# Linear attention and a token/channel mixer: work of batch 2 begun one block sooner, two relus moved to VectorE

## The chip, the cores and the metric

The kernel runs on one core of a Trainium2 chip. A core has five engines with a queue of instructions each: TensorE (PE in the profile; its weight loads are shown as PEld), VectorE (DVE), ScalarE (ACT), GpSimd (POOL) and SyncE (SP, which here only issues transfers). Each engine works through its own queue in order and waits on semaphores for the others. The metric is the time of one execution in device microseconds, as a median over runs; smaller is better.

## What is computed

Eight batches, eight heads, 576 positions, head size 64. Linear attention, whose output is rearranged to (8, 576, 512), and a mixer over positions and then over channels:

```python
def phi(x): return np.where(x > 0, x, np.exp(x) - 1.0) + 1.0
q_p, k_p = phi(q), phi(k)
kv  = einsum('bhsd,bhse->bhde', k_p, v);   z = sum(k_p, axis=2)
x   = einsum('bhsd,bhde->bhse', q_p, kv) / (einsum('bhsd,bhd->bhs', q_p, z) + 1e-6)
x   = x.transpose(0, 2, 1, 3).reshape(8, 576, 512)
h   = maximum(x.transpose(0, 2, 1) @ w_tok1, 0) @ w_tok2      # w_tok1: 576 x 256
u   = x + h.transpose(0, 2, 1)
out = u + maximum(u @ w_ch1, 0) @ w_ch2                        # w_ch1: 512 x 1536
```

## The kernel before

The 576 positions of a batch are split in nine groups of 64 (T = 9): four pairs, which make four tiles of 128 rows (r = 0 to 3), and a tail of 64 (r = 4). The tails of an even and an odd batch share one tile of 128 rows.

For each batch the steps are:
- `phi` (L144) for q and k, in two halves g of four heads each: an exp on ScalarE (`e`, L125), then on VectorE `y` = x + 1 (L131), min(e, 1) (L139) and max of the two (L140) into `qp` or `kp`. `y` has one buffer, `e` has four.
- `vcast` (L149): v to bf16 in `vs`, in two halves; the first on ScalarE, the second on VectorE.
- `kv` (L162): 72 small matmuls, 36 for each half of the heads, and two copies to `kvbd` on ScalarE.
- q transposed into `qT`: for batch 1 by TensorE (`qtr`, L190), from batch 2 on by two DMA transposes issued from SyncE (`qtr_dma`, L197).
- `nd` (L228), six times: four (or two) matmuls on TensorE, then den, reciprocal and a product on VectorE (L219, L221, L222), which give `x`.
- `mm1` (L242): ten matmuls of 128x512 and two relus on ScalarE. `mm2` (L253) for rows 0-1, 2-3 and the tail: matmuls, then an addition on VectorE (L273, L269) into `u` or `ut`. For batch 1 `mm2_half` (L276) does this with the addition of L293.
- u transposed into `uT`: by DMA (`utr_dma`, L457; the tail `utt`, L463), for batches 0 and 1 by TensorE.
- `mm3` (L469): 12 blocks mc of four 128x512 matmuls, each closed by a relu, on ScalarE (L482) or, with `dve=True`, on VectorE (L479), into `cr`. `mm3_tail` (L484) does the tail of two batches in three groups. `mm4` (L495): for each tile of rows t, three slots of four matmuls, then an addition on VectorE (L518, tail L528) into `o_sb`, stored by transfers that GpSimd issues (SyncE and ScalarE in the last pair).

The order is written out by hand. A block's `big` list (the slots) holds the mm3, mm3_tail and mm4 steps of one batch; `fill` holds pairs (slot, step) of later batches' work, and `run` (L668) calls each `big` step and behind it the fill steps of its slot. That order is the order in every engine's queue. Block 0 works on mm3 and mm4 of batch 0 and holds all of batch 1's attention; block 1 (L709-724) has 30 slots: 12 of mm3 for batch 1 (0 to 11), 3 of the tail (12 to 14) and 15 of mm4 (15 to 29, t = 4 to 8). It holds the attention of batch 2 and the phi of batch 3. Its first mm3 steps (mc 0 to 2) are half done before it begins. The dictionaries `at0`, `at1`, `AT3`, `AT` give the slots of the named steps.

On chip the accumulators come from two pools: four banks (`ps_big`) that mm3, mm3_tail and mm4 take in turn, and two buffers of two banks (`ps_sm`) for kv, nd, mm1, mm2. A step that needs a bank waits until the step that had it has been read out. `raw` (the loaded q, k, v) has two sets, one for even and one for odd batches; the six loads of batch n + 2 can go when batch n's have been read. `qp`, `kp` and `vs` have one buffer each.

Of the kernel before, what the change touches and what calls it, by code (L numbers as in the profile page):

```python
# [18 lines left out]
def kernel(  # L19
# [20 lines left out]
    nc = tc.nc  # L40
# [13 lines left out]
    NCH = DCH // 128  # L54
# [54 lines left out]
    def load(nm, n, c, gate=None):  # L109
        src_ = src[nm][n].rearrange("(j a) (p t) d -> (a p) j (t d)", a=2, t=T)  # L110
        js = slice(2 * c, 2 * c + 2)
        return after(nc.sync.dma_start(out=raw[nm, n % 2][:, js], in_=src_[:, js]), gate)
# [9 lines left out]
    def phi_exp(nm, n, j0, nj):  # L122
        f = raw[nm, n % 2][:, j0:j0 + nj].rearrange("p j f -> p (j f)")
        e = work.tile([128, 2 * TD], BF16, name="e", tag="e", bufs=4)[:, :nj * TD]
        nc.scalar.activation(out=e, in_=f, func=AF.Exp)  # L125
        live["e", j0] = e

    def phi_add(nm, n, j0, nj):
        f = raw[nm, n % 2][:, j0:j0 + nj].rearrange("p j f -> p (j f)")
        y = work.tile([128, 2 * TD], BF16, name="y", tag="y", bufs=1)[:, :nj * TD]  # L130
        nc.vector.tensor_scalar(out=y, in0=f, scalar1=1.0, scalar2=None, op0=ALU.add)  # L131
        for j in range(nj):
            live["y", j0 + j] = y[:, j * TD:]

    def phi_end(nm, n, j0, nj):
        c, i = divmod(j0, 2)
        dst = (kp if nm == "k" else qp)[:, c, :, i:i + nj]
        e, y = live["e", j0], live["y", j0][:, :nj * TD]
        nc.vector.tensor_scalar(out=e, in0=e, scalar1=1.0, scalar2=None, op0=ALU.min)  # L139
        nc.vector.tensor_tensor(  # L140
            out=dst.transpose([0, 2, 1, 3]), in0=e.rearrange("p (i t d) -> p i t d", i=nj, t=T),
            in1=y.rearrange("p (i t d) -> p i t d", i=nj, t=T), op=ALU.max)

    def phi(nm, n, c):  # L144
        phi_exp(nm, n, 2 * c, 2)
        phi_add(nm, n, 2 * c, 2)
        phi_end(nm, n, 2 * c, 2)

    def vcast(n, c, copy=nc.scalar.copy):  # L149
        js = slice(2 * c, 2 * c + 2)  # L150
        copy(out=vs[:, js, :, 0:D],  # L151
             in_=raw["v", n % 2][:, js].rearrange("p j (t d) -> p j t d", t=T))
# [9 lines left out]
    def kv(n, cs):  # L162
        b = n % 2
        ps = ps_sm.tile([128, 2, 512], FP32, name="kv_ps", tag="sm")[:, :, 0:2 * D1].rearrange(
            "p a (c e) -> p a c e", c=2)
        for c in cs:
            for t in range(T):
                for a, i in QUARTERS:
                    nc.tensor.matmul(out=ps[half[i], a, c], lhsT=kp[half[a], c, t, i],  # L169
                                     rhs=vs[half[a], 2 * c + i, t],  # L170
                                     start=(t == 0), stop=(t == T - 1))
        cs = slice(cs[0], cs[-1] + 1)
        for i in range(2):
            at = slice(i * D1, (i + 1) * D1)
            nc.scalar.copy(out=kvbd[b][half[i], cs, :, at].transpose([0, 2, 1, 3]),
                           in_=ps[half[i], :, cs])
# [13 lines left out]
    def qtr(n, c, put=nc.scalar.copy):  # L190
        tp = ps_sm.tile([128, 2, 8, 128], BF16, name="tp", tag="sm")
        for h, ts in enumerate(TS):
            qtr_mm(c, ts, tp[:, h])
        for h, ts in enumerate(TS):
            qtr_put(n, c, ts, tp[:, h], put)

    def qtr_dma(n):  # L197
        for a in range(2):
            nc.sync.dma_start_transpose(
                out=qT[n % 2][:, 2 * TD * a:2 * TD * (a + 1)].rearrange("p (f s) -> p f s", s=D),  # L200
                in_=qp[half[a]].rearrange("p c t i d -> p (c t i d)"))
# [26 lines left out]
    def nd(n, g, rs):  # L228
        nd_mm(n, g, rs)
        nd_end(n, g, rs)  # L230
# [215 lines left out]
    def w2_put(kt):  # L446
        nc.scalar.copy(out=w2p[:, TD * kt:TD * (kt + 1)].rearrange("k (t p) -> k t p", t=T),
                       in_=w2r[:, kt].transpose([0, 2, 1]))
# [8 lines left out]
    def utr_dma(n, rs):  # L457
        b = n % 2
        nc.sync.dma_start_transpose(
            out=uT[b][:, rs[0]:rs[0] + len(rs)].rearrange("p r j c -> p (r j) c"),  # L460
            in_=u[b][:, rs[0]:rs[0] + len(rs)].rearrange("p r d -> p (r d)"))
# [7 lines left out]
    def mm3(n, mc, kjs=range(NDM), dve=False):  # L469
        b = n % 2  # L470
        if kjs[0] == 0:
            part_of[mc] = ps_big.tile([128, 512], FP32, name="c_ps", tag="big")
        ps = part_of[mc]
        for kj in kjs:
            nc.tensor.matmul(out=ps, lhsT=wc1[:, kj, 128 * mc:128 * mc + 128],  # L475
                             rhs=uT[b][:, :, kj],
                             start=(kj == 0), stop=(kj == NDM - 1))
        if kjs[-1] == NDM - 1 and dve:
            nc.vector.tensor_scalar(out=cr[b][:, mc, :], in0=ps, scalar1=0.0, scalar2=None,  # L479
                                    op0=ALU.max)  # L480
        elif kjs[-1] == NDM - 1:
            nc.scalar.activation(out=cr[b][:, mc, :], in_=ps, func=AF.Relu)  # L482
# [49 lines left out]
    def prep_k(n, g, copy=nc.scalar.copy):  # L532
        phi("k", n, g)
        vcast(n, g, copy)

    def load_all(n, nms):
        if n < B:
            for nm in nms:
                for g in range(2):
                    load(nm, n, g)  # L540
# [51 lines left out]
    dve, act = nc.vector.tensor_copy, nc.scalar.copy  # L592
# [57 lines left out]
    def steps(n):  # L650

        out_ = [("kv", lambda: kv(n, range(2)))]
        if n == 1:
            puts = [nc.scalar.copy, nc.vector.tensor_copy if n == 1 else nc.scalar.copy]
            out_ += [(f"qt{c}", lambda c=c: qtr(n, c, puts[c])) for c in range(2)]
        for i, rs in enumerate(([0, 1], [2, 3], [4])):
            for g in range(2):
                out_.append((f"nd{i}{g}", lambda g=g, rs=rs: nd(n, g, rs)))
        out_.append(("mm1", lambda: mm1(n)))
        if n > 1:  # L660
            out_ += [("mm2a", lambda: mm2(n, [0, 1])), ("mm2b", lambda: mm2(n, [2, 3])),
                     ("mm2t", lambda: mm2(n, [R]))]
            out_ += [("uta", lambda: utr_dma(n, [0, 1])), ("utb", lambda: utr_dma(n, [2, 3]))]
            if n % 2:
                out_.append(("utt", lambda: utr_tail_dma(n // 2)))
        return out_

    def run(bigs, fill):  # L668
# [5 lines left out]
        for s, fn in fill:  # L674
            assert s < len(bigs)

    m3 = lambda n, k0=0: [lambda mc=mc: mm3(n, mc) for mc in range(k0, NCH)]
    m3t = [lambda i=i: mm3_tail(i) for i in range(3)]
    m4 = lambda p, ts: [lambda t=t, i=i: mm4(p, t, range(4 * i, 4 * i + 4))
                        for t in ts for i in range(3)]  # L680
# [6 lines left out]
    big = [lambda mc=mc: mm3(0, mc, range(2, 4)) for mc in range(3)] + \  # L687
# [4 lines left out]
    fill = [(2, mm2_first_tail)]  # L692
# [4 lines left out]
                 (en, lambda nm=nm, c=c: phi_end(nm, 1, 2 * c, 2))]  # L697
    late = [("vc", lambda: vcast(1, 0)), ("vc", lambda: vcast(1, 1, nc.vector.tensor_copy))]
    fill += [(16 + kt, lambda kt=kt: w2_put(kt)) for kt in range(NT)]
    first = steps(1)  # L700
    for nm, fn in first[1:3] + late + first[0:1] + first[3:]:
        fill += [(at0[nm], fn)]
# [7 lines left out]
    for mc in range(3):  # L710
        mm3(1, mc, range(0, 2))
    utr_tail(0)
    big = [lambda mc=mc: mm3(1, mc, range(2, 4)) for mc in range(3)] + m3(1, 3) + m3t + m4(0, [4, 5, 6, 7, 8])
    at1 = {"kv": 11, "nd00": 13, "nd01": 14, "nd10": 15, "nd11": 16, "nd20": 17, "nd21": 18,
           "mm1": 20, "mm2a": 21, "mm2b": 22, "mm2t": 24, "uta": 21, "utb": 22}
    fill = [(s, lambda g=g: phi("q", 2, g)) for g, s in ((0, 0), (1, 2))]
    fill += [(3, lambda: qtr_dma(2)), (3, lambda: load_all(3, "qkv"))]
    fill += [(s, lambda g=g: phi("k", 2, g)) for g, s in ((0, 4), (1, 6))]
    fill += [(8, lambda: vcast(2, 0)), (9, lambda: vcast(2, 1, nc.vector.tensor_copy))]
    fill += [(at1[nm], fn) for nm, fn in steps(2)]  # L720
    fill += [(s, lambda g=g: phi("q", 3, g)) for g, s in ((0, 19), (1, 23))]
    fill += [(24, lambda: qtr_dma(3)), (24, lambda: load_all(4, "qkv"))]
    fill += [(s, lambda g=g: prep_k(3, g)) for g, s in ((0, 25), (1, 27))]
    run(big, sorted(fill, key=lambda e: e[0]))

    AT3 = {"kv": 1, "nd00": 3, "nd01": 4, "nd10": 5, "nd11": 6, "nd20": 7, "nd21": 8,
# [3 lines left out]
    for n in range(2, B):  # L730
        p, b = divmod(n, 2)
        if b == 0:
            big = m3(n) + m4(p, [0, 1, 2, 3])
        else:
            big = m3(n) + m3t + m4(p, [4, 5, 6, 7, 8] if n + 1 < B else [8, 4, 5, 6, 7])
        fill = []
# [40 lines left out]
```

## Time and profile before

| | |
|---|---|
| time, median of 7 runs | 268.23 us (267.40 to 268.55) |
| the profiled execution's own time | 268.46 us |
| its span, first to last instruction | 266.7 us |
| granted clock of TensorE, mean | 0.997 |
| last slots of block 0: last kc step of mm4 for batch 0 ends | 50.85 us |
| block 1: first slot begins | 56.74 us |
| kv of batch 2 begins | 67.22 us |
| mm1 of batch 2 begins | 76.98 us |
| block 2: first slot begins | 89.32 us |
| kv of batch 3 begins | 91.14 us |
| loads of q of batch 2: issued, and time to landing | 36.6 and 37.0 us, 6.0 and 6.8 us |

Times within the execution are counted from the start of the span. In a timeline each row is a run of like instructions: start, duration, engine, line of the kernel, operation, what is written from what is read, size, count, and in brackets the idle time of the engine ahead of it and what ended that. TensorE starts the next matmul before the last one has left it, so its rows overlap, and the start-to-start distance is the pace; the same holds, less so, for VectorE and ScalarE. A few per cent of the matmul records are missing, which shows as a hole of one matmul's length in a row.

### The profile page before, as it was taken

How to read it: one execution, taken by the hardware profiler on the slowest of the kernel's cores; microseconds unless marked ns; L12 is line 12 of the kernel's file. 1: busy time of each engine (PE TensorE's matmuls, PEld its weight loads, DVE VectorE, ACT ScalarE, POOL GpSimd, SP SyncE). 2: the span in 40 equal slices, each digit the busy share in tenths (PEclk: the TensorE clock that was granted, in tenths of full speed). 3: DMA queues.
4: the chain of work that ended last, by engine and by line, in shares of the span. 5: the costliest groups of instructions: out<-in, count | busy, mean ns of one | idle time of the engine just before them, and what ended most of it. 6: DMA issues, size and time to landing. Idle time of an engine off the chain costs nothing.

```text
span 266.7 us, 5122 instructions
## 1 busy us (share of the span) xinstructions
PE 255.9 (96%) x2088; PEld 134.1 (50%) x2107; DVE 157.4 (59%) x309; ACT 133.0 (50%) x202; POOL 32.4 (12%) x54
## 2 busy tenths in 40 slices
PE   7998989999999999999999999999999999999992
PEld 3684445553744454445464554445554554444641
DVE  5764977469587876948674296938684272420121
ACT  5635764269808368525771358425870353036300
POOL 9720300110000200030001300030001300000000
PEclk9999999999999999999999999999999999999998
DMA  7999999253957695799999990671067500730042
GB/s 261 247 203 288 366 223 403 97 132 97 337 209 154 154 385 204 86 224 349 312 409 235 266 407 27 141 164 43 2 129 120 118 2 0 157 99 2 0 118 79
DMA packets 49927, 48.34 MB, mean 181 GB/s; under 512 B 30256, under 2 KB 35248, under 8 KB 49904
## 3 DMA queue, kind: packets, MB, share of 16 engines
q1 hardware_dynamic: 41824, 35.53, 45.9%
q0 software_dynamic: 7440, 11.44, 20.1%
q10 hardware_dynamic: 640, 1.05, 1.2%
q8 instruction: 16, 0.26, 0.4%
q14 instruction: 7, 0.06, 0.1%
HBM read 35.85 MB, written 9.44 MB: 170 GB/s over the span
## 4 chain that ended last, share of the span: by engine, by line
PE 80%; DVE 7%; DMA 4%; ACT 4%; issue 3%; POOL 0%; ACTq 0%; POOLq 0%
PE h_ps L501 32%; PE c_ps L475 21%; PE a_ps L248 5%; PE h_ps L261 4%; PE c_ps L489 4%; DMA uTt<-ut 4%; PE bank L545 3%; PE nd_ps L210 3%; PE kv_ps L169 2%; DVE y L131 2%; ACT cr L482 1%; ACT e L125 1%; DVE e L139 1%; DVE kp L140 1%; PE bank L363 1%
## 5 line engine op out<-in xcount | busy, mean ns | idle before, releaser
L475 PE MATMUL c_ps<-uT,wc 128*128 128x512 bf16 x384 | 91.3, 379 | 0.7 <-ACT uT L444 0.4
L482 ACT ACTIVATE cr<-c_ps 128x512 bf16<-128x512 f32 x93 | 54.4, 603 | 74.1 <-PE c_ps L475 74.0
L501 PE MATMUL h_ps<-wc,cr 128*128 128x512 bf16 x377 | 87.4, 379 | 0.5
L501 PEld LDWEIGHTS <-cr 128*128 128x128 bf16 x384 | 37.0, 98 | 42.0
L475 PEld LDWEIGHTS <-wc 128*128 128x128 bf16 x384 | 35.8, 98 | 37.8 <-issue 1.9
L518 DVE TENSOR_TENSOR o_sb<-h_ps,u 128x512 f32<-128x512 f32 x32 | 21.8, 688 | 27.3 <-PE h_ps L501 25.6
L523 POOL DMA_DIRECT2D out_dram<-o_sb x24 | 14.5, 609 | 156.1 <-DVE o_sb L518 156.1
L222 DVE TENSOR_TENSOR x<-nd_ps,den 128x512 bf16<-128x512 f32 (+1 forms) x42 | 25.3, 602 | 1.5
L139 DVE TENSOR_SCALAR e<-e 128x1152 bf16<-128x1152 bf16 x30 | 13.9, 463 | 12.5 <-ACT e L125 12.4
L125 ACT ACTIVATE e<-k_raw 128x1152 bf16<-128x1152 f32 x16 | 18.8, 1173 | 2.3 <-DMA k_raw<-in_k_dram 2.3
L273 DVE TENSOR_TENSOR u<-h_ps,x 128x1024 bf16<-128x1024 f32 x12 | 14.4, 1220 | 9.2 <-PE h_ps L261 9.2
L125 ACT ACTIVATE e<-q_raw 128x1152 bf16<-128x1152 f32 x16 | 18.6, 1161 | 1.1 <-DMA q_raw<-in_q_dram 1.1
L219 DVE TENSOR_SCALAR den<-nd_ps 128x8 f32<-128x8 f32 (+1 forms) x42 | 6.8, 163 | 19.3 <-PE nd_ps L210 18.7
L251 ACT ACTIVATE ar<-a_ps 128x512 bf16<-128x512 f32 x14 | 7.6, 594 | 18.1 <-PE a_ps L248 18.1
L210 PEld LDWEIGHTS <-qT 128*128 128x128 bf16 x140 | 11.4, 98 | 9.5 <-issue 0.2
L261 PE MATMUL h_ps<-ar,w2p 128*128 128x512 bf16 x57 | 15.6, 379 | 0.1
L210 PE MATMUL nd_ps<-kvbd,qT 128*128 128x130 bf16 x140 | 15.1, 223 | 0.0
L248 PE MATMUL a_ps<-x,w 128*128 128x512 bf16 x50 | 13.9, 379 | 0.3
L151 ACT CAST vs<-v_raw 128x1152 bf16<-128x1152 f32 x12 | 13.9, 1162 | 0.0
L528 DVE TENSOR_TENSOR o_sb<-h_ps,ut 128x512 f32<-128x512 f32 x4 | 2.8, 689 | 18.7 <-PE h_ps L501 18.7
L131 DVE TENSOR_SCALAR y<-q_raw 128x1152 bf16<-128x1152 f32 x16 | 12.4, 773 | 0.3
L140 DVE TENSOR_TENSOR qp<-e,y 128x1152 bf16<-128x1152 bf16 x16 | 12.1, 759 | 0.6
(102 smaller groups left out, 215.7 us busy)
## 6 DMA issues: line engine op xcount, KB each, us to landing
k_raw<-in_k_dram SPq DMA_DIRECT2D x16, 576.0 KB, 8.9
q_raw<-in_q_dram SPq DMA_DIRECT2D x16, 576.0 KB, 6.8
v_raw<-in_v_dram SPq DMA_DIRECT2D x14, 576.0 KB, 10.9
out_dram<-o_sb POOLq DMA_DIRECT2D x24, 256.0 KB, 3.8
wc<-in_moe_w_ch_dram POOLq DMA_DIRECT2D x8, 384.0 KB, 9.3
out_dram<-o_sb SPq DMA_DIRECT2D x10, 128.0 KB, 2.3
out_dram<-o_sb ACTq DMA_DIRECT2D x8, 128.0 KB, 2.6
out_dram<-o_sb POOLq DMA_DIRECT2D x6, 128.0 KB, 6.9
```

What stands on the lines that cost most here:

```text
L125: nc.scalar.activation(out=e, in_=f, func=AF.Exp)
L131: nc.vector.tensor_scalar(out=y, in0=f, scalar1=1.0, scalar2=None, op0=ALU.add)
L139: nc.vector.tensor_scalar(out=e, in0=e, scalar1=1.0, scalar2=None, op0=ALU.min)
L140: nc.vector.tensor_tensor(out=dst.transpose([0, 2, 1, 3]), in0=e.rearrange("p (i t d) -> p i t d", i=nj, t=T), in1=y.rearrange("p (i t d) ...
L210: nc.tensor.matmul(out=o[:, a], lhsT=qT[b][:, t0:t0 + 128], rhs=kvbd[b][:, c, a], start=True, stop=True)
L222: nc.vector.tensor_tensor(out=x[b][:, rs[0]:rs[0] + m, HG * D * g:HG * D * (g + 1)].rearrange("p r (h d) -> p r h d", h=HG), in0=v_[:, :, ...
L248: nc.tensor.matmul(out=ps[:, mt], lhsT=w1t[:, b, ms] if r == R else w1[:, r, ms], rhs=x[b][:, r, :], start=(r == 0), stop=(r == R))
L261: nc.tensor.matmul(out=ps[:, i], lhsT=w2v(kt, r, b), rhs=ar[b][:, kt, :], start=(kt == 0), stop=(kt == NT - 1 and not add))
L475: nc.tensor.matmul(out=ps, lhsT=wc1[:, kj, 128 * mc:128 * mc + 128], rhs=uT[b][:, :, kj], start=(kj == 0), stop=(kj == NDM - 1))
L482: nc.scalar.activation(out=cr[b][:, mc, :], in_=ps, func=AF.Relu)
L501: nc.tensor.matmul(out=ps, lhsT=crt[:, kc, :] if t == 8 else cr[b][:, kc, 128 * r:128 * r + 128], rhs=wc2[:, kc, :], start=(kc == 0), stop ...
L518: nc.vector.tensor_tensor(out=o, in0=ps, in1=u[b][:, r, :], op=ALU.add)
```

## The change

Three edits, none of which alters what is computed.

1. The two halves of phi of q of batch 2 move from slots 0 and 2 of block 1 to slot 21 of block 0, behind batch 1's last nd step (slot 20) and ahead of its mm1 (slot 21). The two transposing transfers of q of batch 2 and the six loads of batch 3 move from slot 3 of block 1 to slot 22 of block 0.
2. In block 1 the rest of batch 2 moves up: the phi of k from slots 4 and 6 to 0 and 2, the casts of v from 8 and 9 to 4 and 5, kv from 11 to 7, the nd steps from 13, 14, 15, 16, 17, 18 to 9 to 14, mm1 from 20 to 16, mm2 from 21, 22, 24 to 17, 18, 20 with the transfers of u. Batch 3's phi of q goes from slots 19 and 23 to 19 and 21, its transposes and the loads of batch 4 from 24 to 22, its phi of k and casts from 25 and 27 to 24 and 26.
3. The relus of mc 4 and mc 7 of batch 1 go from ScalarE (L482) to VectorE (L479).

In the queues this means: TensorE has the same instructions, with kv, nd, mm1 and mm2 of batch 2 further ahead among the mm3 and mm4 steps. GpSimd's and SyncE's queues hold the same instructions in the same order. ScalarE's two exps of q of batch 2 stand behind the w2p copies of block 0 and ahead of batch 1's mm1 relus. VectorE's six instructions of that phi stand behind the last nd step of batch 1 and ahead of the first two output additions of batch 0 (L518); in block 1 the relu of mc 4 stands ahead of the cast of v's second half, the relu of mc 7 behind it.

```diff
     fill += [(16 + kt, lambda kt=kt: w2_put(kt)) for kt in range(NT)]
+    fill += [(21, lambda g=g: phi("q", 2, g)) for g in range(2)]
+    fill += [(22, lambda: qtr_dma(2)), (22, lambda: load_all(3, "qkv"))]
     first = steps(1)
...
-    big = [lambda mc=mc: mm3(1, mc, range(2, 4)) for mc in range(3)] + m3(1, 3) + m3t + m4(0, [4, 5, 6, 7, 8])
-    at1 = {"kv": 11, "nd00": 13, "nd01": 14, "nd10": 15, "nd11": 16, "nd20": 17, "nd21": 18,
-           "mm1": 20, "mm2a": 21, "mm2b": 22, "mm2t": 24, "uta": 21, "utb": 22}
-    fill = [(s, lambda g=g: phi("q", 2, g)) for g, s in ((0, 0), (1, 2))]
-    fill += [(3, lambda: qtr_dma(2)), (3, lambda: load_all(3, "qkv"))]
-    fill += [(s, lambda g=g: phi("k", 2, g)) for g, s in ((0, 4), (1, 6))]
-    fill += [(8, lambda: vcast(2, 0)), (9, lambda: vcast(2, 1, nc.vector.tensor_copy))]
+    big = [lambda mc=mc: mm3(1, mc, range(2, 4)) for mc in range(3)] + [lambda mc=mc: mm3(1, mc, dve=mc in (4, 7)) for mc in range(3, NCH)] + m3t + m4(0, [4, 5, 6, 7, 8])
+    at1 = {"kv": 7, "nd00": 9, "nd01": 10, "nd10": 11, "nd11": 12, "nd20": 13, "nd21": 14,
+           "mm1": 16, "mm2a": 17, "mm2b": 18, "mm2t": 20, "uta": 17, "utb": 18}
+    fill = [(s, lambda g=g: phi("k", 2, g)) for g, s in ((0, 0), (1, 2))]
+    fill += [(4, lambda: vcast(2, 0)), (5, lambda: vcast(2, 1, nc.vector.tensor_copy))]
     fill += [(at1[nm], fn) for nm, fn in steps(2)]
-    fill += [(s, lambda g=g: phi("q", 3, g)) for g, s in ((0, 19), (1, 23))]
-    fill += [(24, lambda: qtr_dma(3)), (24, lambda: load_all(4, "qkv"))]
-    fill += [(s, lambda g=g: prep_k(3, g)) for g, s in ((0, 25), (1, 27))]
+    fill += [(s, lambda g=g: phi("q", 3, g)) for g, s in ((0, 19), (1, 21))]
+    fill += [(22, lambda: qtr_dma(3)), (22, lambda: load_all(4, "qkv"))]
+    fill += [(s, lambda g=g: prep_k(3, g)) for g, s in ((0, 24), (1, 26))]
```

## The prediction

> **What bounds the kernel.** The page first: its parts 1 and 4.
>
> ```profile
> span 266.7 us, 5122 instructions
> ...
> PE 255.9 (96%) x2088; PEld 134.1 (50%) x2107; DVE 157.4 (59%) x309; ACT 133.0 (50%) x202; POOL 32.4 (12%) x54
> ...
> PE 80%; DVE 7%; DMA 4%; ACT 4%; issue 3%; POOL 0%; ACTq 0%; POOLq 0%
> ```
>
> TensorE is the bound. The diff neither adds nor removes a matmul, so it can only win or lose places where TensorE stands still. I therefore read TensorE's timeline from the end of batch 0's block to the first slots of batch 2's.
>
> ```profile
> 56.74 9.98 PE L475 MATMUL c_ps<-uT,wc 128*128 128x512 bf16 x42
> 67.22 0.78 PE L169 MATMUL kv_ps<-vs,kp 64*64 64x65 bf16 x72 [0.51 <-ACT vs L151]
> ...
> 89.32 1.89 PE L475 MATMUL c_ps<-uT,wc 128*128 128x512 bf16 x8
> 91.14 1.07 PE L169 MATMUL kv_ps<-vs,kp 64*64 64x65 bf16 x72
> ...
> 117.59 0.78 PE L169 MATMUL kv_ps<-vs,kp 64*64 64x65 bf16 x72
> 118.30 1.90 PE L475 MATMUL c_ps<-uT,wc 128*128 128x512 bf16 x8
> ```
>
> The pace of a 128x512 matmul is (1.89 - 0.38) / 7 = 0.216 (0.38 is the mean of one on the page), so four are 0.863. An undisturbed kv, batch 4's, takes 118.30 - 117.59 = 0.71, and 0.09 passes in front of it. Against that:
> - the 42 matmuls at 56.74 should take 41 x 0.216 + 0.38 = 9.22 and take 9.98. The starts of the single ones put the missing 0.76 ahead of mc 7 (61.64, 0.15 late), mc 9 (63.67, 0.30) and mc 11 (65.69, 0.30);
> - kv of batch 2 (67.22) starts 0.67 behind the last matmul's slot, 0.58 beyond the usual 0.09;
> - kv of batch 3 (91.14) takes 1.07 instead of 0.78: 0.28 lost in its middle.
>
> Together 1.62 us. Between them there is only 0.26 at 80.5, where mm2a waits for the relu of mm1; that distance isn't altered. ScalarE shows what holds block 1 up:
>
> ```profile
> 57.42 0.60 ACT L482 ACTIVATE cr<-c_ps 128x512 bf16<-128x512 f32 x1
> 57.91 1.17 ACT L125 ACTIVATE e<-q_raw 128x1152 bf16<-128x1152 f32 x1
> 58.96 1.09 ACT L482 ACTIVATE cr<-c_ps 128x512 bf16<-128x512 f32 x2
> 59.92 1.18 ACT L125 ACTIVATE e<-q_raw 128x1152 bf16<-128x1152 f32 x1
> 60.97 1.11 ACT L482 ACTIVATE cr<-c_ps 128x512 bf16<-128x512 f32 x2
> ...
> 65.94 1.23 ACT L151 CAST vs<-v_raw 128x1152 bf16<-128x1152 f32 x1
> ```
>
> From 57.4 to 69 it has no gap. One relu moves it on by 0.48, an exp or a cast by 1.05. With four banks, mc 7 needs the relu of mc 3, which ends 61.57; mc 9 and mc 11 need those of mc 5 and mc 7; kv needs the cast that ends 67.17. Then VectorE:
>
> ```profile
> 46.71 0.42 DVE L222 TENSOR_TENSOR x<-nd_ps,den 128x256 bf16<-128x256 f32 x1
> 50.40 1.29 DVE L518 TENSOR_TENSOR o_sb<-h_ps,u 128x512 f32<-128x512 f32 x2 [3.27 <-PE h_ps L501]
> 52.14 0.69 DVE L293 TENSOR_TENSOR u<-h_ps,x 128x512 bf16<-128x512 f32 x1 [0.45 <-PE h_ps L288]
> ...
> 59.10 0.46 DVE L139 TENSOR_SCALAR e<-e 128x1152 bf16<-128x1152 bf16 x1 [1.82 <-ACT e L125]
> 59.60 0.76 DVE L140 TENSOR_TENSOR qp<-e,y 128x1152 bf16<-128x1152 bf16 x1
> 60.39 0.76 DVE L131 TENSOR_SCALAR y<-q_raw 128x1152 bf16<-128x1152 f32 x1
> ...
> 90.91 0.76 DVE L140 TENSOR_TENSOR kp<-e,y 128x1152 bf16<-128x1152 bf16 x1
> ```
>
> Idle for 3.27 ahead of 50.40; the last row is batch 3's kp, ready at 91.67, which kv of batch 3 waits for.
>
> **Part 1: phi of q of batch 2 into block 0.** On ScalarE two exps, 2 x 1.05, go behind the w2p copies (end 42.99), where nothing runs until 49.32. Their input is issued at 36.56 and 37.05 and lands 6.0 and 6.8 later, 42.6 and 43.9. So they run from 43.0 to 45.2: cost nothing, and 4 us of cover before the relu of mm1 behind them would be late. On VectorE six instructions go in front of the first o_sb addition. From the neighbouring rows: y starts 0.34 after the last x (47.05), min 0.67 later, max 0.49, the next y 0.80 (it must wait for max, y has one buffer), then 0.67, 0.49 and 0.67: 47.05 + 3.79 = 50.84. The two additions start 0.44 late and hand over at 50.84 + 2 x 0.61 = 52.06; L293, which TensorE releases at 52.14 anyway, isn't late. Cover left: 0.08 there, and 0.10 more before L293's bank is wanted (52.83 against 52.99). Beyond 0.18, every us is paid in full: mm2_half, the transposes and block 1 follow. An unknown duration here would be a y at 1.01 (the one at 31.83) and a min at 0.58 (90.30), twice each: 0.76 more, 0.58 on the path. Both of those rows lie beside transfers being issued by GpSimd, which issues none from 33.1 to 52.0, so I take zero, and keep 0.58 for the range. On SyncE nothing changes places, but qtr_dma(2) (2 issues) and the six loads of batch 3 go out at 51 instead of 62.5: the DMA engines are idle from 50 to 52 and little used to 66, and the buffers were last read at 39.2. Zero.
>
> **Part 2: block 1.** Up to mc 3 the new ScalarE order repeats the old one, with exps of k for those of q, so mc 7 starts at 61.64 again, 0.15 lost, and ends its slot at 62.50. Then kv. ScalarE: the relu of mc 4 is now VectorE's, so the cast of v's first half follows the relu of mc 3: 60.97 + 0.48 = 61.45, ready at 62.65. VectorE: min 59.10, max 59.60, y 60.39, min 61.13, max 61.62 (the old rows, now for k), the relu of mc 4 at 62.29 and 0.60 later (as behind the relu at 29.95) the cast of the second half, 62.89 + 0.76 = 63.65. So TensorE does half of kv from 62.70, waits from 63.06 for 63.70, does the second half, and is at mc 8 at 63.70 + 0.36 + 0.11 = 64.17. Undisturbed that would be 62.50 + 0.09 + 0.71 = 63.30: 0.87 lost. Behind it, the relus of mc 5 and 6 end at 63.6 and the banks of mc 8 to 11 are free in time; an nd step costs VectorE 1.10 and comes every 0.863 + 0.235 = 1.10, as in batch 2's block (94 to 99, no wait).
> Before 0.76 + 0.58 = 1.34, now 0.15 + 0.87 = 1.02: **0.32 gained**. Bounds: if the second cast came as early as the first, only 0.15 + 0.2 would stay (gain 1.0); if the y and min ahead of it took 1.01 and 0.58 as above, it comes 0.37 later (gain -0.05).
>
> **Part 3: batch 3's kp.** Everything from mm1 on stands four slots (3.5 us) sooner in the same work. Counted on from 64.17, mm2b ends at 79.05, and VectorE goes on by the steps of 83.05 to 91.67: L273 at 79.26, q's two phis from 80.40 and 83.42 with two additions between, k's from 85.85 and 88.28, last kp ready at 90.2. Block 2 starts at 88.98, its kv at 90.8, its second half at 91.15: 0.95 to spare. **0.28 gained.**
> One addition now lands so that GpSimd issues stores (about 83 to 84.3) beside the y at 83.42. The row for that is 1.01 instead of 0.76, 0.25 out of a margin of 0.95. The Trainium skill, "SBUF — State Buffer", section "Who interferes with whom", says that VectorE in a two-port mode and GpSimd exclude each other for a whole instruction; by that rule the y could wait out an issue (0.61 in this trace), still inside the margin. Rule and row thus give the same sum here.
>
> **Sum.** 0.32 + 0.28 = 0.60. The execution of 268.46 (span 266.7 plus 1.8 around it) would take 267.86; it stands 0.23 above the median, and 268.23 - 0.60 = **267.6**.
>
> **Rivals.**
> *Hidden later* (about 268.2). Block 3 has a stall of its own: uTt lands at 132.5 and TensorE stands from 132.0. If that landing keeps its clock time, TensorE waits 0.6 longer and all is given back: 268.23. For it: the transfer takes 10.8 behind six loads. Against: SyncE's sequence starts with the transposes of u at 108.04, released by VectorE's L273, that is by TensorE, after DMA engines idle for 3 us; it moves along. Half given back: 267.9.
> *Less stall* (about 267.0). The wait inside kv falls away, as it would with the cast early: 268.23 - 1.0 - 0.28 = 266.95. Against: VectorE is strictly in order, and the relu stands in front.
> *Slower* (about 268.8). kv of batch 2 now stands ahead of four mc steps that need nothing from it. Its second cast hangs on a VectorE chain of six steps from 59.10 to 63.65. If the cast ends later than 63.65 + 0.60 = 64.25, the change loses. For it: the chain's rows vary (y 0.75 to 1.01, min 0.44 to 0.58). Against: 0.37 is all that those rows give, and GpSimd is quiet from 58.1 on. The price is one for one: 1.2 us late gives 268.23 - 0.60 + 1.2 = 268.8.
> *It doesn't matter*: block 1's gain at its lower bound leaves 0.28 - 0.05: 268.0.
>
> **From cases to numbers.** As worked out 0.50 (267.3 to 267.9), given back or at the lower bound 0.24, less stall 0.11, slower than before 0.15. A measurement of this kernel tells 0.2%, 0.54 us, from no change: below 267.69 is faster, above 268.77 slower. The likeliest time lies just below the first line, so two fifths of its case (0.20) count as same, as do three quarters of the given-back cases (0.18) and a third of the slower one (0.05): faster 0.30 + 0.11 + 0.06 = 0.47, same 0.43, slower 0.10. Range 266.9 to 268.4: from the less-stall case to most of the lower bounds, 0.58 of part 1 among them.
>
> **What would show it.** Right: exps of q ahead of L251 at 43 to 45; TensorE's first matmul of block 1 still at 56.74; kv of batch 2 at 62.7, parted by a wait for the cast on VectorE of some 0.6; mc 9 and mc 11 without delay; block 2 from 89.0; kv of batch 3 in 0.78; everything later shifted by 0.6, the wait for uTt still about 0.5. Wrong: L293 later than 52.2; a wait at mc 8 or after; uTt's wait grown to 1 us; or a stall of kv other than 0.9.

## The result, and the profile after

| | before | after |
|---|---|---|
| median, runs taken side by side | 268.46 us (72 runs) | 267.57 us (30 runs) |
| ratio, with its 95% interval | | 0.9964 (0.9953 to 0.9974) |
| profiled execution, span | 266.7 us | 266.1 us |
| first matmul of mm2_half (end of block 0) starts | 50.85 us | 51.42 us |

The change gains 0.97 us (268.46 x 0.0036), with an interval of 0.70 to 1.26. Gains in time are given this way below, from the ratio; the two medians themselves differ by 0.89. The page of the changed kernel:

```profile
span 266.1 us, 5123 instructions
...
PE 255.1 (96%) x2088; PEld 134.1 (50%) x2107; DVE 158.7 (60%) x311; ACT 132.8 (50%) x200; POOL 33.3 (13%) x54
...
PE 85%; DVE 6%; DMA 3%; ACT 2%; issue 1%; POOL 1%; ACTq 0%; POOLq 0%
```

The chain that ended last goes through TensorE for 85% instead of 80%: some detours over ScalarE and VectorE are gone. The two spans differ by 0.5 only, because the stage up to mm2_half, in which the change gives TensorE nothing to wait for, took 0.57 longer in this execution: TensorE waited 0.9 us for one of the first loads (`cr<-in_v_dram`), a wait that the profile before doesn't show. The end of that stage, the start of mm2_half, varies from 50.25 to 51.52 among the profiles of this study, with 50.85 to 51.15 for the kernel before and 50.95 to 51.42 for the changed one. So stages are compared by their own length here, from the start of one matmul to the start of another. TensorE's timeline after:

```profile
57.30 5.92 PE L475 MATMUL c_ps<-uT,wc 128*128 128x512 bf16 x26
63.24 0.48 PE L169 MATMUL kv_ps<-vs,kp 64*64 64x65 bf16 x36
64.27 0.48 PE L169 MATMUL kv_ps<-vs,kp 64*64 64x65 bf16 x36 [0.55 <-DVE vs L151]
64.69 1.90 PE L475 MATMUL c_ps<-uT,wc 128*128 128x512 bf16 x8
...
89.53 1.89 PE L475 MATMUL c_ps<-uT,wc 128*128 128x512 bf16 x8
91.35 0.78 PE L169 MATMUL kv_ps<-vs,kp 64*64 64x65 bf16 x72
92.06 1.25 PE L475 MATMUL c_ps<-uT,wc 128*128 128x512 bf16 x5
```

kv of batch 2 is now in two pieces of 36, with a hole from 63.54 to 64.27 while it waits for the cast on VectorE. The 26 matmuls ahead of it take 5.92, where 25 x 0.216 + 0.38 = 5.78 are needed: the 0.15 ahead of mc 7 is still there. kv of batch 3 takes 0.78, its hole is gone. VectorE and ScalarE after:

```profile
50.73 0.76 DVE L140 TENSOR_TENSOR qp<-e,y 128x1152 bf16<-128x1152 bf16 x1
51.41 1.28 DVE L518 TENSOR_TENSOR o_sb<-h_ps,u 128x512 f32<-128x512 f32 x2
52.71 0.69 DVE L293 TENSOR_TENSOR u<-h_ps,x 128x512 bf16<-128x512 f32 x1
...
62.19 0.76 DVE L140 TENSOR_TENSOR kp<-e,y 128x1152 bf16<-128x1152 bf16 x1
62.87 0.68 DVE L479 TENSOR_SCALAR cr<-c_ps 128x512 bf16<-128x512 f32 x1
63.47 0.75 DVE L151 CAST vs<-v_raw 128x1152 bf16<-128x1152 f32 x1
...
90.11 0.76 DVE L140 TENSOR_TENSOR kp<-e,y 128x1152 bf16<-128x1152 bf16 x1
```

```profile
44.00 1.16 ACT L125 ACTIVATE e<-q_raw 128x1152 bf16<-128x1152 f32 x1 [0.45 <-DVE den L219]
45.39 1.16 ACT L125 ACTIVATE e<-q_raw 128x1152 bf16<-128x1152 f32 x1 [0.23 <-DVE den L221]
49.89 1.09 ACT L251 ACTIVATE ar<-a_ps 128x512 bf16<-128x512 f32 x2 [3.33 <-PE a_ps L248]
...
61.53 0.62 ACT L482 ACTIVATE cr<-c_ps 128x512 bf16<-128x512 f32 x1
62.01 1.18 ACT L151 CAST vs<-v_raw 128x1152 bf16<-128x1152 f32 x1
```

The relu of mc 4 (62.87) stands in front of the cast (63.47 to 64.22), and kv's second half starts 0.05 behind the end of the cast. The moved exps wait for their loads (landed 43.92 and 45.31; the releaser that the view names is not what they read) and are done 3.3 ahead of the relu of mm1. L293 starts at 52.71, 1.29 behind the start of mm2_half, exactly as before (52.14 against 50.85).

By stage (my differences of matmul starts, us): "block 1" runs from the transposes of batch 0's tail to the last matmul ahead of block 2, "block 2" from there to the first mm3_tail matmul that needs uTt, "rest" from there to the last matmul.

| kernel | block 1 | block 2 | rest | ratio to before (95%) |
|---|---|---|---|---|
| before | 32.59 | 43.45 | 129.05 | |
| after | 32.24 | 42.71 | 129.06 | 0.9964 (0.9953 to 0.9974) |
| block 0's edit alone | 31.27 | 43.28 | 129.06 | 0.9942 (0.9920 to 0.9965) |
| after, no relu on VectorE | 31.99 | 42.62 | 129.06 | 0.9960 (0.9939 to 0.9980) |
| after, kv one slot later | 31.95 | 42.76 | 129.06 | 0.9974 (0.9951 to 0.9997) |
| after, both of these | 31.41 | 42.76 | 129.06 | 0.9954 (0.9932 to 0.9975) |
| before, uTt first | 32.58 | 42.91 | 129.06 | 0.9991 (0.9972 to 1.0011) |
| after, uTt first | 32.24 | 42.62 | 129.06 | 0.9955 (0.9934 to 0.9976) |
| batch 3's steps alone | 32.59 | 42.62 | 129.06 | 0.9976 (0.9958 to 0.9994) |
| against every wait | 31.16 | 42.62 | 129.06 | 0.9917 (0.9893 to 0.9941) |
| before, again; a third time | 32.59; 32.58 | 43.05; 46.79 | 129.06; 129.06 | 0.9999 (0.9978 to 1.0021); 0.9998 (0.9975 to 1.0020) |
| after, again; a third time | 32.24; 32.24 | 42.63; 42.62 | 129.06; 129.06 | 0.9976 (0.9953 to 0.9999); 0.9971 (0.9950 to 0.9991) |

Block 1 gives 0.35 and block 2 0.74 in the first pair of profiles. Block 1 repeats to 0.01 in every further profile of the same kernel. Block 2 doesn't, and that is the wait for uTt, the transposed tail of batches 2 and 3, which a transfer brings and which the first mm3_tail of block 3 reads. (The 46.79 of the third profile of the kernel before has another cause, told below.) The two further measurements of the changed kernel give 0.64 and 0.78 us, with wider intervals (0.03 to 1.26 and 0.24 to 1.34). The row of the kernel before, and of the kernel after, with the first mm3_tail of block 3:

```profile
132.55 1.05 PE L489 MATMUL c_ps<-uTt,wc 128*128 128x128 bf16 x16 [0.38 <-DMA uTt<-ut]
```

```profile
132.03 1.05 PE L489 MATMUL c_ps<-uTt,wc 128*128 128x128 bf16 x16
```

The first has TensorE idle for 0.38 in front of it. That number counts from the end of the last matmul, which the profile models; by the starts TensorE loses 0.54. The second shows nothing, and loses 0.09 by the starts: 0.45 that the prediction hadn't counted.

### The profile page after: what moved, and what is told of

It is laid out like the page before. It is cut to its first block, busy times and chain, and to the rows that moved or that the text cites. A ratio compares the mean times of both kernels' runs of the same rounds, so it can differ in the third digit from the quotient of the medians.

```text
span 266.1 us, 5123 instructions
## 1 busy us (share of the span) xinstructions
PE 255.1 (96%) x2088; PEld 134.1 (50%) x2107; DVE 158.7 (60%) x311; ACT 132.8 (50%) x200; POOL 33.3 (13%) x54
## 4 chain that ended last, share of the span: by engine, by line
PE 85%; DVE 6%; DMA 3%; ACT 2%; issue 1%; POOL 1%; ACTq 0%; POOLq 0%
PE h_ps L501 34%; PE c_ps L475 26%; PE a_ps L248 5%; PE h_ps L261 5%; PE c_ps L489 4%; PE nd_ps L210 3%; DMA cr<-in_v_dram 3%; PE kv_ps L169 2%; DVE y L131 1%; DVE cr L479 1%; DVE kp L140 1%; PE bank L363 1%; PE bank L413 1%; DVE e L139 1%; POOL qT L564 1%
## 5 line engine op out<-in xcount | busy, mean ns | idle before, releaser
L482 ACT ACTIVATE cr<-c_ps 128x512 bf16<-128x512 f32 x91 | 53.5, 599 | 78.0 <-PE c_ps L475 77.8
L518 DVE TENSOR_TENSOR o_sb<-h_ps,u 128x512 f32<-128x512 f32 x32 | 21.8, 688 | 28.0 <-PE h_ps L501 26.3
L139 DVE TENSOR_SCALAR e<-e 128x1152 bf16<-128x1152 bf16 x30 | 14.1, 471 | 12.4 <-ACT e L125 12.3
L273 DVE TENSOR_TENSOR u<-h_ps,x 128x1024 bf16<-128x1024 f32 x12 | 14.3, 1219 | 7.1 <-PE h_ps L261 7.1
```

The costliest lines, as they stand in the source:

```text
L518: nc.vector.tensor_tensor(out=o, in0=ps, in1=u[b][:, r, :], op=ALU.add)
```

## The experiments

**Which edit does it: block 0's alone.** All of block 1 stays in its old slots, only without the phi of q.

```diff
+    fill += [(21, lambda g=g: phi("q", 2, g)) for g in range(2)]
+    fill += [(22, lambda: qtr_dma(2)), (22, lambda: load_all(3, "qkv"))]
...
-    fill = [(s, lambda g=g: phi("q", 2, g)) for g, s in ((0, 0), (1, 2))]
-    fill += [(3, lambda: qtr_dma(2)), (3, lambda: load_all(3, "qkv"))]
-    fill += [(s, lambda g=g: phi("k", 2, g)) for g, s in ((0, 4), (1, 6))]
+    fill = [(s, lambda g=g: phi("k", 2, g)) for g, s in ((0, 4), (1, 6))]
```

> Block 0's edit alone: phi of q of batch 2 in block 0, all slots of block 1 as before, no relu on VectorE. Theory (the two exps of q were what made ScalarE late in block 1): the waits ahead of mc 7, 9, 11 (0.15 + 0.30 + 0.30) and of kv of batch 2 (0.58) all go, the wait inside kv of batch 3 (0.28) stays, ratio to the kernel before 0.995 (1.34 us), better than the whole change at 0.9964. Rival (the gain comes from the earlier slots of kv and of batch 3's work): ratio 0.999 to 1.000, and the waits in block 1 stay. uTt's wait in block 3: near 0.5 if it depends on the loads of batch 4, near 0.1 if on those of batch 3, anything if it is chance.

Its TensorE and ScalarE timelines:

```profile
56.81 9.23 PE L475 MATMUL c_ps<-uT,wc 128*128 128x512 bf16 x42
65.97 0.78 PE L169 MATMUL kv_ps<-vs,kp 64*64 64x65 bf16 x72
...
89.89 1.07 PE L169 MATMUL kv_ps<-vs,kp 64*64 64x65 bf16 x72
```

```profile
57.49 2.27 ACT L482 ACTIVATE cr<-c_ps 128x512 bf16<-128x512 f32 x4
60.03 0.60 ACT L482 ACTIVATE cr<-c_ps 128x512 bf16<-128x512 f32 x1 [0.27 <-PE c_ps L475]
60.53 1.15 ACT L125 ACTIVATE e<-k_raw 128x1152 bf16<-128x1152 f32 x1
```

The 42 matmuls take 9.23 (9.98 before), kv follows without a hole, and ScalarE now waits for TensorE (0.27 at 60.03) and not the other way round. Block 1 is 1.32 shorter, the time 1.56 (0.94 to 2.15). kv of batch 3 keeps its hole (1.07), as expected. So block 0's edit alone removes every wait of block 1 but the 0.26 at mm2, which none of the edits alters here. What the change does on top of that in block 1 puts 0.97 back (32.24 against 31.27); the next three runs show which part of it does that. The wait for uTt is 0.36 here, between the values that were written down ahead for its two cases.

**The relus on VectorE.** The changed kernel with `dve=False` for mc 4 and mc 7.

(The start of the line is left out, "..." in both.)

```diff
-    ... mm3(1, mc, dve=mc in (4, 7)) for mc in range(3, NCH)] + m3t + m4(0, [4, 5, 6, 7, 8])
+    ... mm3(1, mc, dve=False) for mc in range(3, NCH)] + m3t + m4(0, [4, 5, 6, 7, 8])
```

> The changed kernel with all twelve relus of batch 1 on ScalarE again. Theory (kv of batch 2 waits for the cast on VectorE, and the relu of mc 4 in front of it costs 0.6 of that): VectorE's cast ends 0.6 sooner, ScalarE's first cast 0.48 later; kv starts some 0.45 later than in the changed kernel and runs through in 0.78, mc 8 starts 0.25 to 0.3 sooner; ratio to the kernel before about 0.9954, 0.001 better than the changed kernel. Rival (the two relus on VectorE relieve ScalarE, and without them mc 9 to 11 wait for banks): 0.3 to 0.6 us slower than the changed kernel, ratio 0.998.

kv on TensorE, and the cast on VectorE:

```profile
62.76 0.78 PE L169 MATMUL kv_ps<-vs,kp 64*64 64x65 bf16 x72 [0.51 <-ACT vs L151]
63.47 1.90 PE L475 MATMUL c_ps<-uT,wc 128*128 128x512 bf16 x8
```

```profile
61.22 0.76 DVE L140 TENSOR_TENSOR kp<-e,y 128x1152 bf16<-128x1152 bf16 x1
61.90 0.76 DVE L151 CAST vs<-v_raw 128x1152 bf16<-128x1152 f32 x1
```

There is one wait of 0.51 ahead of kv (0.58 by the starts), now for ScalarE, instead of the one inside it. Block 1 is 0.25 shorter than in the changed kernel, the amount the theory gave, and no wait follows at mc 9 to 11: the rival is out. The two relus on VectorE cost 0.25 where they stand. In time the gain over the changed kernel, 0.0004 of the ratio, is inside the intervals.

**kv one slot later.** kv 8, nd 10 to 15, mm1 17, mm2 18, 19, 21; everything else as in the changed kernel.

```diff
-    at1 = {"kv": 7, "nd00": 9, "nd01": 10, "nd10": 11, "nd11": 12, "nd20": 13, "nd21": 14,
-           "mm1": 16, "mm2a": 17, "mm2b": 18, "mm2t": 20, "uta": 17, "utb": 18}
+    at1 = {"kv": 8, "nd00": 10, "nd01": 11, "nd10": 12, "nd11": 13, "nd20": 14, "nd21": 15,
+           "mm1": 17, "mm2a": 18, "mm2b": 19, "mm2t": 21, "uta": 18, "utb": 19}
```

> The changed kernel with kv, nd, mm1 and mm2 of batch 2 one slot (0.86) later, relus of mc 4 and 7 still on VectorE. Theory (VectorE's queue is what is late: mc 8 then needs the bank of mc 4, whose relu on VectorE ends only about 0.4 after TensorE comes to mc 8): the wait of 0.7 inside kv goes, one of 0.4 to 0.5 ahead of mc 8 comes in its place, kv of batch 3 loses up to 0.1; ratio about 0.995 to 0.996. Rival (only kv's slot is too early): no wait ahead of mc 8, gain of 0.8 over the changed kernel, ratio 0.9934.

TensorE's timeline of this run:

```profile
56.42 5.92 PE L475 MATMUL c_ps<-uT,wc 128*128 128x512 bf16 x26
62.72 1.02 PE L475 MATMUL c_ps<-uT,wc 128*128 128x512 bf16 x4 [0.38 <-DVE cr L479]
63.68 0.78 PE L169 MATMUL kv_ps<-vs,kp 64*64 64x65 bf16 x72
```

kv runs through, and mc 8 stands in front of it, waiting for the relu of mc 4 on VectorE (0.54 by the starts, 0.38 by the modelled ends). The rival is out: it isn't kv's slot alone, it is VectorE's queue, whose late instruction simply hits another matmul. Block 1 is 0.29 shorter than in the changed kernel. kv of batch 3 loses 0.14, a little more than the 0.1 allowed for. The measured ratio, 0.9974, lies above the 0.995 to 0.996 expected; its interval, 0.9951 to 0.9997, holds most of that range.

**Both.** The two edits above together.

> Both: kv and what follows of batch 2 one slot later, and all relus of batch 1 on ScalarE. Theory: no wait in kv of batch 2 nor ahead of mc 8; of block 1's waits only 0.15 ahead of mc 7 and 0.26 at mm2 stay, at most 0.1 in kv of batch 3; 0.8 better than the changed kernel, ratio 0.9934. Rival (ScalarE becomes late again with twelve relus): waits of 0.3 at mc 9 and 11, ratio 0.996.

```profile
56.33 6.79 PE L475 MATMUL c_ps<-uT,wc 128*128 128x512 bf16 x30
63.04 0.78 PE L169 MATMUL kv_ps<-vs,kp 64*64 64x65 bf16 x72
...
89.56 0.92 PE L169 MATMUL kv_ps<-vs,kp 64*64 64x65 bf16 x72
```

No wait in kv of batch 2 or at mc 8 (30 matmuls in 6.79: 29 x 0.216 + 0.38 = 6.64, the 0.15 at mc 7 again). Block 1 is 0.83 shorter than in the changed kernel, as expected. kv of batch 3 loses 0.14; mm2, and with it VectorE's chain for batch 3, is a slot later, which is the likely reason. Together the four kernels part the 0.97 that the change puts back on top of block 0's edit: 0.14 for batch 2's steps moved up with kv in slot 8 (31.41 against 31.27, the wait at mc 7), 0.58 for kv and what follows it one slot earlier (31.99 against 31.41), 0.25 for the two relus (32.24 against 31.99). In time only 0.0010 of 0.003 showed: the interval (0.9932 to 0.9975) reaches the 0.9934 expected at its edge.

**Batch 3's steps alone.** The kernel before, with only the slots of batch 3 in block 1 moved.

```diff
-    fill += [(s, lambda g=g: phi("q", 3, g)) for g, s in ((0, 19), (1, 23))]
-    fill += [(24, lambda: qtr_dma(3)), (24, lambda: load_all(4, "qkv"))]
-    fill += [(s, lambda g=g: prep_k(3, g)) for g, s in ((0, 25), (1, 27))]
+    fill += [(s, lambda g=g: phi("q", 3, g)) for g, s in ((0, 19), (1, 21))]
+    fill += [(22, lambda: qtr_dma(3)), (22, lambda: load_all(4, "qkv"))]
+    fill += [(s, lambda g=g: prep_k(3, g)) for g, s in ((0, 24), (1, 26))]
```

> The kernel before with only batch 3's steps in block 1 moved: phi of q from slots 19 and 23 to 19 and 21, its transposes and the loads of batch 4 from 24 to 22, phi of k and casts from 25 and 27 to 24 and 26. Theory: VectorE uses the 0.5 it stood idle between the two additions of mm2, the last kp is ready 0.5 sooner, the 0.28 inside kv of batch 3 goes, block 1's waits stay: ratio 0.999. On uTt: if the wait for it depends on where batch 3's steps and the loads of batch 4 stand, it is 0.1 or less and the ratio 0.997; if not, it is 0.3 to 0.8.

TensorE's timeline of this run:

```profile
66.62 0.78 PE L169 MATMUL kv_ps<-vs,kp 64*64 64x65 bf16 x72 [0.51 <-ACT vs L151]
...
90.54 0.78 PE L169 MATMUL kv_ps<-vs,kp 64*64 64x65 bf16 x72
```

Block 1 keeps all its waits, kv of batch 3 loses its hole, and there is no wait for uTt: block 2 is 0.83 shorter than in the first profile of the kernel before, 0.28 of it kv. In this execution the slots of batch 3 alone do all that the change does in block 2; the earlier mm2 isn't needed for it. The ratio, 0.9976 (0.9958 to 0.9994), lies near the 0.997 expected for this case, but its interval holds the 0.999 as well.

**What uTt is worth.** In block 2 SyncE issues the transpose of the tail, uTt, behind the six loads of batch 5. One edit, on the kernel before and on the changed one, turns that round:

```diff
-                fill += [(12 + d, lambda: load_all(5, "qkv"))]
+                fill += [(16, lambda: load_all(5, "qkv"))]
```

> The kernel before, with the six loads of batch 5 issued behind the transpose of the tail (uTt) in block 2 instead of ahead of it. It measures what the wait for uTt in block 3 is worth in time. Theory (uTt lands late because SyncE issues it behind six loads in a stretch in which the transfer engines are full): uTt lands 6 us or more ahead of its use, the wait of 0.5 goes, nothing else moves; ratio to the kernel before 0.998. Rival (a later load of batch 5 holds up block 3, or uTt lands as late as before): ratio 1.000 or above, a wait in block 3 or 4.

> The changed kernel with the same edit. Theory A (the changed kernel gains 0.45 over the worked-out 0.6 because uTt lands just in time in it): only 0.1 more to gain, ratio to the kernel before 0.996. Theory B (the profiled execution was a lucky one, and the wait for uTt is there in most executions of the changed kernel): 0.4 to 0.5 more, ratio 0.9945.

In both, uTt lands 12 us ahead of its use and the wait is gone (block 2 at 42.91 with kv's hole, 42.62 without). In time the kernel before gains 0.24 (interval -0.30 to 0.75), the changed one, at 0.9955, 0.24 over its 0.9964, well inside the intervals. Theory A's 0.996 and B's 0.9945 both lie in the interval of the second run, so the times don't part them; the further profiles do.

**Chance or not: both kernels again.** The same two programs, each profiled twice more.

> The kernel before, unchanged, for another look at when uTt lands in block 3. Theory (where batch 3's steps stand in block 1 decides it): a wait of 0.3 to 0.6 again, as in the first profile of this kernel and in the run of block 0's edit alone. Rival (chance: the landing varies by a us between executions of one kernel): any value from 0 to 0.6. Ratio 1.000.

> The same kernel a third time. Theory: a wait for uTt of 0.3 to 0.6. Rival: any value from 0 to 0.6. Ratio 1.000.

> The changed kernel again. Theory (batch 3's steps decide): a wait for uTt of 0 to 0.1. Rival (chance): any value from 0 to 0.6. The waits in block 1 (0.15, 0.09 + 0.73) and the time from the first matmul of mm2_half to the end without uTt's wait as in its first profile; ratio 0.9964.

> The changed kernel a third time. Theory: a wait for uTt of 0 to 0.1. Rival: any value from 0 to 0.6. Ratio 0.9964.

Landing of uTt, counted from the start of kv of batch 4 (needed at 14.42):

| batch 3's steps in block 1 | landings, us |
|---|---|
| old slots | 14.9 and 14.5 (before), 14.7 (block 0's edit alone) |
| new slots | 14.5, 14.2, 14.0 (after), 14.4, 12.9, 14.1 (its three variants), 14.3 (batch 3's steps alone) |

In the third profile of the kernel before, an execution of 272.05 us, TensorE stands still for 2.0 us at a stretch in block 3, waiting for another transfer, the transposed q of batch 4 (`qT`), so that uTt's wait can't be read there and it isn't in the table. The wait for uTt is 0.54, 0.14 and 0.36 with the old slots and 0.09 or nothing in all seven with the new ones. That agrees with the theory that batch 3's steps decide; its "0.3 to 0.6" for the old slots missed once, at 0.14. The landing varies by some tenths between executions of one kernel, and every landing with the new slots is earlier than every one with the old, the closest by 0.04. Ten profiles make it likely, not certain, that the slots of batch 3 move it. Why they would isn't settled: SyncE's chain in block 2 starts at the same time relative to TensorE in all of them (transposes of u 9.55 ahead of kv of batch 4), the transfer engines are idle ahead of it where that was read, and the order of what follows is the same. The difference shows first at the second transposing transfer of q of batch 4, ahead of the loads: it lands 1.6 to 2.2 us behind the start of that kv in the three profiles of the upper row and from 1.3 ahead to 1.4 behind in the seven of the lower. What moves that transfer isn't shown.

**Against every wait at once.** Block 0's edit, kv in slot 8, all relus on ScalarE, mm2 two slots behind mm1, one half of batch 3's phi of q ahead of mm1, uTt first. Of the edit against the changed kernel only the new slots are printed; the relus and the loads of batch 5 are set as in the runs above.

```diff
...
+    at1 = {"kv": 8, "nd00": 10, "nd01": 11, "nd10": 12, "nd11": 13, "nd20": 14, "nd21": 15,
+           "mm1": 17, "mm2a": 19, "mm2b": 20, "mm2t": 21, "uta": 19, "utb": 20}
...
+    fill += [(s, lambda g=g: phi("q", 3, g)) for g, s in ((0, 16), (1, 21))]
...
```

> A version against every wait found: block 0's edit; kv of batch 2 in slot 8, all relus of batch 1 on ScalarE; mm2 two slots behind mm1 instead of one; the first half of batch 3's phi of q ahead of mm1; uTt ahead of the loads of batch 5. Theory: of 1.34 in block 1 only 0.15 ahead of mc 7 stays, 0.26 at mm2, 0.28 in kv of batch 3 and 0.54 at uTt go: 2.27 us, ratio to the kernel before 0.9915. Rival (a wait comes up elsewhere, in kv of batch 3 or at u's transposes for block 2): 0.994 to 0.996.

The waits of TensorE between 53.5 and 140 (in total, times, longest) in the changed kernel, then in this one:

```profile
PE kv_ps L169 <- DVE vs L151: 0.5, 1, 0.5
PE tp L304 <- ACT u L291: 0.2, 1, 0.2
```

```profile
PE tp L304 <- ACT u L291: 0.2, 1, 0.2
```

What is left is the last wait of block 0, which every kernel here has. Waits as short as the 0.15 at mc 7, in both kernels, and the 0.26 at mm2, in the changed one, don't show in this view. Median 266.38, ratio 0.9917 (0.9893 to 0.9941) against 0.9915 expected: 2.2 us faster than the kernel before, 1.3 faster than the change. Block 1 takes 31.16 and block 2 42.62. It beats both, and no wait came up elsewhere.

## Why the prediction was right, point by point

The predicted time, 267.6, and the measured median, 267.57, agree. That is closer than the steps deserve: the ratio's gain is 0.97, the sum was 0.60, and the 0.60 lies just outside the interval of 0.70 to 1.26. The predicted time was set from a median of 268.23 over seven runs; with 72 it is 268.46, and the two errors nearly cancel: the agreement to 0.03 is luck. The two further measurements, 0.64 and 0.78, hold 0.60 in their intervals; it is the stages of the profiles that say which terms were right.

- **Part 1, no cost in block 0:** right. From the first matmul of mm2_half to block 1 takes 5.66 with and without it. L293 isn't late; the 0.08 of cover held. The first exp started at 44.00, 1.0 later than worked out (0.43 beyond the 0.57 by which this execution is late there), since its loads were issued later (37.9 and 38.4 us); the cover took that, and 3.3 us were left. The step had it as "cost nothing", and left out that it is itself the gain: alone it takes 1.32 out of block 1, more than the whole change does.
- **Part 2, 0.32 gained in block 1:** right, 0.35. The waits were to be 0.15 at mc 7 and 0.87 at kv; they are 0.15 and 0.82 (0.09 ahead of kv's first half, 0.73 between the halves). The 0.05 too much is kv's second half, counted at 0.47 and measured at 0.42. The cause is shown: without the relu in front of the cast the wait changes engines and shrinks by 0.25; with kv a slot later it moves to mc 8.
- **Part 3, 0.28 gained in kv of batch 3:** right, to the hundredth, and shown apart from the rest by the run of batch 3's steps alone. The last kp is ready at 90.87, 0.80 ahead of the start of kv's second half at 91.67; 0.95 was worked out. The collision of that y with GpSimd's stores came, and VectorE paid nothing for it: y took 0.74 at 83.97. GpSimd paid: the two issues beside y took 1.68 instead of 1.20, as the timelines of both engines after show:

```profile
83.97 0.74 DVE L131 TENSOR_SCALAR y<-q_raw 128x1152 bf16<-128x1152 f32 x1
```

```profile
83.75 1.68 POOL L523 DMA_DIRECT2D out_dram<-o_sb  x2 [25.07 <-DVE o_sb L518]
89.21 1.20 POOL L523 DMA_DIRECT2D out_dram<-o_sb  x2 [3.77 <-DVE o_sb L518]
```

  That one of the two engines is held up and the other isn't agrees with the Trainium skill, "SBUF — State Buffer", section "Who interferes with whom". Its rule that the one which issues first holds the shared ports for its whole instruction doesn't fit this row: the issue starts at 83.75, y at 83.97. (Spans on GpSimd are rough in this profile, but the row repeats: in all seven profiles with y 0.22 behind the start of an issue, y took 0.74 and that issue 1.08 or 1.09.)
- **The rival "hidden later" and its premise:** the step that was wrong. "It moves along" was right for the start of SyncE's chain and left the wait for uTt at 0.5 in the sum. In the changed kernel it is 0.09, 0 and 0. The term, put at no change, was mis-sized by 0.05 to 0.54, depending on the executions compared (0.54 and 0.14 in the kernel before), on the side opposite to the rival. 0.35 + 0.28 and an estimated mean of 0.3 for it (0.34 less 0.03) make 0.93, which the 0.97 measured fits.
- **The rival "slower":** its point of decision, a cast at 64.25, wasn't reached; on the same count the cast ended at 63.65, as worked out.
- **The rival "less stall":** out for the change, but the runs show that its 1.0 in block 1 was to be had (1.18, 32.59 against 31.41), by taking the relus off VectorE and kv one slot back.

## What to carry to other kernels

When an engine in the middle is late for a stretch, move work out of that stretch into one where it idles, and stop there: pulling the consumer forward in the same step can spend the cover that was just won (1.32 gained; 0.97 given back, 0.58 of it because kv stood one slot too early). A step handed from a full queue to an emptier one has to be placed against what stands behind it in the new queue; here a relu that nobody needed soon stood in front of a cast that TensorE was waiting for. A transfer that lands within half a us of its use is a term of the sum with a width of its own: a single profile gives it a size that the next one doesn't repeat.

## What was unexpected of the hardware

- Compute stages repeat to 0.01 us between executions (block 1 at 32.58 to 32.59 and at 32.24 in three profiles each), while a stretch of transfers of 24 us varies at its end by 0.4 and 0.5 us among the profiles of one kernel and by 2 among all ten (uTt lands 12.9 to 14.9 behind the same matmul), and the first loads make the start of the steady part vary from 50.25 to 51.52.
- Who pays when VectorE and GpSimd's issue of stores meet isn't fixed: y took 1.01 instead of 0.75 at 31.83 in the kernel before, where two issues followed each other during it, and 0.74 at 83.97 in the changed one, where the issue was stretched by 0.48 instead. What decides it isn't shown.
